# Another order of 1,135 steps in an attention, token-mix and MLP kernel

## The chip, the cores and the metric

One core of a Trainium2 chip runs the whole program as one launch. The metric is device time in microseconds (us) of one launch; before the change the median of three runs is 952.76 us (951.86 to 954.37). TensorE (PE) multiplies, VectorE (DVE), ScalarE (ACT) and GpSimd (POOL) do elementwise work, SyncE (SP) issues all DMAs. Each engine works off its own instruction stream strictly in order and waits on semaphores for the others.

## The reference

```python
scores = where(block_i >= block_j, q @ k.T / sqrt(64), -1e9)   # 4 batches, 8 heads, 576 x 64, blocks of 64
x  = softmax(scores) @ v                                       # -> 4 x 576 x 512
u  = x + (relu(x.T @ w_tok1) @ w_tok2).T                       # token mix, 576 -> 256 -> 576
u2 = u + relu(u @ w_ch1) @ w_ch2                               # MLP 1, 512 -> 1536 -> 512
out = u2 + relu(layernorm(u2) * g @ w_ch1') @ w_ch2'           # MLP 2, 512 -> 2048 -> 512
```

q, k, v are float32; the weights come as float64 and are taken apart into two planes on the chip.

## The kernel before

Every matmul operand is held as a high and a low plane, and each product is three passes (high x high, high x low, low x high). The 32 heads are worked in 16 pairs; two pairs make a quad (8 in all) of 256 columns, on which the token mix runs. `ORDER` is a string of words, each one step; `attention_and_token_mix` calls them one by one under a manual schedule, so the string alone sets the order of the instructions on every engine. A step's number is how often its word has come, or the number behind a colon. Later, `Mlps.run` has loops of its own for the rest of the two MLPs; they are not touched.

The words of one pair p: `lqk`, `lv` load q, k, v (SP). `rlk`, `rlq` copy k (ACT) and q (POOL) into the layout to transpose, `trk`, `trq`, `trr` transpose them on PE, `kh/qh/rmh` (ACT) and `kl/ql/rml` (DVE) write the two planes `kt`. `s3`, `s1`, `s02`, `s4` are the score matmuls by groups of row tiles, into PSUM tiles `ps` (two of them). `m*` is the row maximum (DVE), `n*` its negative (ACT), `e*` the exponential (ACT), `h*`, `l*` the two half-precision planes (POOL or DVE). `tA` and `tB` are DMA transposes of the planes of groups A (`s3`, `s1`) and B (`s02`, `s4`). `a3`, `a1` (from A), `a20`, `a4` (from B) multiply with v. `dn`, `ev`, `ev4` divide into `x`.

The words of one quad q: `xh` (ACT), `xl` (POOL) are the planes `xr` of x, `t1a`, `t1b` the first token matmul, `rh`, `rl` its planes, `t2a/b/c` the second, `ua/ub/uc` (DVE) add x, `us0`, `us1` store u to DRAM. `tl`, `td0` to `td3` load and split one of nine tiles of token weights (`td1` is four DVE operations). For the MLP: `bwl` loads a raw tile of weights, `bw0` takes its size (ACT), `bw1` rebases it (four DVE operations), `bc*` finds a scale, `bw2`, `bw3` write the planes. `bnl`, `ba`, `bk`, `bh`, `bo`, `bt` bring rows of u back and make their transposed planes; `b1` is one first-layer tile (PE), `br`, `bs` its planes.

PSUM tiles of `trk`, `trq`, `trr`, `cmm`, `a4`, `t1`, `t2` and most `b1` share three banks (`ps_mm`). SP, ACT, DVE and POOL never overtake within their stream: a step that waits holds up all behind it.

Of the kernel before, what the change touches and what calls it, by code (L numbers as in the profile page):

```python
# [43 lines left out]


ORDER = """
    lqk lv lt rlk rlq lv trk trq kh lqk abv kl qh cmm trr ql lv rmh rml cd1 s3 abv lt vh rlk rlq vl s1 m3 abv
    n3 cmm m1 trk e3 n1 cd1 trq lqk kh h3 trr e1 kl s4 l3 lv rmh h1 qh rml vh s02 m4 tl ql l1 vl tl rlk n4 rlq
    e4 tA s3 abv m02 td0 n02 td1 e02 lqk cmm trk m3 lv td0 h02 s1 kh n3 cd1 e3 h4 kl tl a3 l4 m1 td2 n1 vh td1
    s02 td3 e1 rlq l02 tl td2 abv td3 vl td0 h3 tB rlk td1 l3 trq td0 h1 trr lqk qh m02 s4 rmh td2 l1 n02 lv  # L50
    rml cmm e02 m4 a1 td3 ql a20 n4 cd1 tA e4 h02 td1 s3 vh h4 rlk l02 l4 td2 tl abv vl td3 s1 tl:6 m3 lv n3
    a4 m1 e3 n1 tl:5 dn ev e1 h3 s02 dn tB td0 l3 h1 td0:6 ev4 td1 abv td1:6 td2 l1 td0:5 a3 m02 td2:6 td3 tA
    s4 td3:6 n02 td1:5 e02 tl trk trq kh h02 m4 trr a1 qh tl a20 kl rmh n4 rlq td2:5 rml e4 a4 td3:5 ql lqk ev
    s3 h4 l02 bwl ev4 xh l4 s1 m3 a3 td0 xl tB trk n3 td0 m1 e3 trq n1 td1 trr a1 kh s02 rmh e1 rlq kl qh h3
    s4 td2 m02 rlk t1a td3 lqk n02 h1 e02 rml l1 bwl m4 t1b ql n4 l3 td1 e4 s3 dn td2 rh dn rlk rl s1 h02 tA
    m3 cmm a4 td3 h4 n3 t2a m1 e3 bwl l4 n1 cd1 l02 cmm a20 e1 h3 s02 ua vh tB l3 h1 ev cd1 a3 ev4 m02 vh t2b
    l1 n02 vl e02 t2c tA ub s4 uc vl trk h02 trq lv kh m4 trr a1 qh rlq a20 kl rmh n4 rml e4 a4 lqk ql ev h4
    s3 l02 l4 ev4 lv xh s1 m3 a3 abv xl us0 cmm n3 trk m1 e3 trq n1 cd1 a1 tB dn trr kh s02 rmh kl e1 rlq rml
    h3 qh t1a m02 abv l3 us1 vh n02 h1 s4 e02 ql t1b m4 l1 vl rlk h02 s3 tA rh rl n4 e4 a4 m3 lqk h4 t2a l4 n3
    l02 e3 s1 lv ua cmm a20 h3 m1 s02 n1 tB ev l3 e1 cd1 dn ev4 a3 h1 vh m02 t2b l1 rlk abv n02 vl s4 e02 tA  # L60
    ub t2c m4 trk uc trq n4 kh lv h02 trr a1 qh kl a20 rmh e4 rlq rml a4 ql h4 lqk ev s3 l4 l02 ev4 xh us0 s1
    m3 a3 xl abv tB cmm n3 trk m1 e3 trq n1 cd1 a1 dn trr kh s02 rmh kl e1 rlq us1 rml h3 qh t1a m02 vh l3 rlk
    n02 h1 lqk s4 e02 ql t1b m4 l1 vl h02 tA s3 rh rl n4 e4 rlq a4 m3 lv h4 t2a l4 n3 l02 e3 s1 ua cmm a20 h3
    m1 s02 tB n1 ev l3 e1 cd1 dn ev4 a3 h1 abv m02 t2b l1 vh n02 vl e02 t2c tA ub trk s4 uc kh h02 trq lv m4
    trr a1 qh kl n4 a20 rmh e4 rml a4 ql us0 rlk h4 ev s3 l4 l02 ev4 lqk xh s1 m3 a3 abv xl tB cmm n3 trk m1
    e3 trq n1 cd1 a1 dn trr kh s02 rmh kl e1 rlq us1 rml h3 qh t1a m02 vh l3 rlk n02 h1 lqk s4 e02 ql t1b m4
    l1 vl h02 s3 tA rh rl n4 rlq e4 a4 m3 h4 lv t2a l4 n3 l02 e3 s1 ua cmm a20 h3 m1 s02 tB n1 ev l3 e1 cd1 dn
    ev4 a3 h1 abv m02 t2b l1 vh n02 vl e02 t2c tA ub trk s4 uc kh h02 trq lv m4 trr a1 qh kl n4 a20 rmh e4 rml
    a4 ql us0 rlk h4 ev s1 l4 l02 ev4 s3 lqk xh m1 a3 n1 abv m3 xl tB cmm trk e1 trq n3 cd1 a1 kh dn trr s02
    e3 kl rlq us1 rmh h3 qh rml t1a m02 vh l3 rlk n02 h1 s4 lqk e02 ql t1b m4 l1 vl s3 h02 rh tA rl n4 rlq e4  # L70
    a4 m3 h4 lv t2a n3 l02 l4 e3 s1 ua cmm a20 h3 m1 s02 tB n1 ev l3 e1 cd1 dn ev4 a3 h1 abv m02 t2b l1 vh n02
    vl e02 t2c tA ub trk s4 uc kh h02 trq us0 m4 trr a1 qh kl n4 a20 rmh e4 rml a4 ql rlk h4 ev s3 lqk l4 l02
    ev4 xh s1 m3 us1 tB a3 xl cmm n3 trk m1 e3 trq n1 cd1 a1 dn trr kh s02 rmh kl e1 h3 rml qh t1a l3 h1 vh
    m02 rlk s4 n02 ql e02 l1 t1b m4 vl n4 tA rlq e4 s3 h02 rh dn h4 rl s1 m3 l4 t2a n3 m1 e3 cmm a4 ua n1 a20
    cd1 e1 h3 l02 s02 vh l3 h1 tB ev s4 m02 ev4 a3 l1 t2b n02 m4 e02 vl tA n4 t2c ub trk e4 uc trq kh trr us0
    dn h02 a1 rmh a20 kl qh h4 rml a4 ql l4 ev s3 l02 ev4 xh s1 m3 a3 us1 n3 a1 m1 tB bnl bnl bnl bnl bw0:0 e3
    n1 e1 xl s02 h3 s4 l3 h1 l1 tA t1a m02 n02 m4 bw1:0 e02 n4 t1b e4 h02 rh a4 h4 l02 l4 rl tB a20 ev4 ev dn
    t2a bw0:1 ba ba ba ba bw1:1 ua t2b ub t2c uc a3 a1 a20 a4 ev xh0 us0 us1 bk xl0 ev4 xh1 xl1 pc t1a bnl bnl
    bnl bnl bh bh bw0:2 bh bh bo bo bo bo bt bt bt bt bw1:2 t1b rh rl t2a bw0:3 bw1:3 bc1 ua t2b t2c bc2 ub uc
    us0 us1 op bnl bnl bnl bnl ba ba ba ba bk bc3 bw2 bw3 bw2 bw3 bw2 bw3 bw2 bw3 b1 br bh bh bo bo bt bt bs  # L80
    b1 br bh bh bo bo bt bt bs bw0:4 bw1:4 b1 br ba ba ba ba bs bk b1 br bh bh bo bo bt bt bs b1 br bh bh bo
    bo bt bt bs bw0:5 bw1:5 b1 br bs bw0:6 bw1:6 bnl bnl bnl bnl b1 br bs b1 br bs bw0:7 bw1:7 b1 br bc1 bs b1
    br bs bc2 b1 br bc3 bs bw2 bw3 bw2 bw3 ba ba ba ba b1 br bs bw2 bw3 bw2 bw3 bk
"""


class Net:
# [1043 lines left out]
```

## Time and profile before

| what | value |
|---|---|
| median of three runs | 952.76 us (951.86 to 954.37) |
| profiled execution | 954.12 us, span 952.3 us |
| mean granted TensorE clock | 0.966 of full |
| PE busy in the span | 881.7 us (93%) |
| DVE, ACT, POOL busy | 644.0, 352.4, 210.8 us |
| last exponentials of pair 15 | about 249 us |
| first `b1` matmul | 278.39 us |

Read it by stages. From about 330 us to the end PE works almost without a gap on the MLPs. Before, the span is the phase that `ORDER` sets. Times in the rows are microseconds from the start of the span; "<-" in a wait names what it waited for; a line number is that of the kernel before.

### The profile page before, as it was taken

The page shows a single profiled execution, that of the slowest core. Times are in us where ns is not written, and L with a number is a line of the kernel's source. Part 1 is how long each engine was busy: PE and PEld are TensorE (multiplying, and loading weights), DVE is VectorE, ACT ScalarE, POOL GpSimd, SP SyncE. Part 2 cuts the span into 40 slices and gives each one's busy share as a digit, 9 for nine tenths or more (in the row PEclk, how much of TensorE's full clock was granted, in tenths as well). Part 3 has the DMA queues.
Part 4 walks back from the last instruction along what each step waited for, and adds up shares of the span by engine and source line. Part 5 has one row for each costly group of instructions (what it writes and reads, how often), then busy time and mean ns, then how long its engine had stood idle before and what let it go on. Part 6 is the DMA issues. An engine that isn't in the chain of part 4 may idle for free.

```text
span 952.3 us, 15126 instructions
## 1 busy us (share of the span) xinstructions
PE 881.7 (93%) x5924; PEld 506.6 (53%) x5924; DVE 644.0 (68%) x1249; ACT 352.4 (37%) x847; POOL 210.8 (22%) x187
## 2 busy tenths in 40 slices
...
GB/s 201 183 202 178 208 201 207 163 215 156 202 207 220 81 167 86 76 58 89 67 44 51 83 89 67 111 45 45 45 44 45 23 1 1 1 1 10 58 56 77
DMA packets 193479, 96.66 MB, mean 102 GB/s; under 512 B 167744, under 2 KB 180800, under 8 KB 193408
## 3 DMA queue, kind: packets, MB, share of 16 engines
...
## 4 chain that ended last, share of the span: by engine, by line
PE 41%; issue 30%; POOL 2%; DVE 1%; ACT 0%; POOLq 0%
PE psy L984 21%; PE mm L947 20%; POOL pl L932 1%; POOL pl L931 1%; POOL vr L913 0%; POOL hlB L418 0%; DVE z L924 0%; ACT wide L398 0%; PE ps L333 0%; PE mm L812 0%; PE ps L363 0%; DVE diag L808 0%; DVE acc L988 0%; DVE mxf L801 0%; DVE mxf L802 0%
## 5 line engine op out<-in xcount | busy, mean ns | idle before, releaser
L947 PE MATMUL mm<-xt,w 128*128 128x512 f16 (+1 forms) x1680 | 335.5, 359 | 4.5 <-ACT w L848 2.6
L984 PE MATMUL psy<-w,hid 128*128 128x512 f16 x1512 | 335.5, 381 | 2.4 <-ACT w L848 2.0
L947 PEld LDWEIGHTS <-w 128*128 128x128 f16 x1680 | 164.6, 98 | 169.0 <-issue 4.4
L984 PEld LDWEIGHTS <-hid 128*128 128x128 f16 x1512 | 148.7, 98 | 180.5 <-issue 6.3
L958 ACT ACTIVATE hid<-mm 128x512 f16<-128x512 f32 (+1 forms) x140 | 77.3, 554 | 386.8 <-PE mm L947 386.7
L961 DVE SCALAR_TENSOR_TENSOR hid<-mm,hid 128x512 f16<-128x512 f32 (+1 forms) x140 | 87.9, 634 | 127.4 <-ACT hid L958 127.4
L988 DVE SCALAR_TENSOR_TENSOR acc<-psy,rg,acc 128x512 f32<-128x512 f32 x72 | 53.9, 750 | 87.5 <-PE psy L984 87.5
L333 PE MATMUL ps<-kt 64*128 64x512 f32 (+3 forms) x384 | 54.9, 402 | 17.8 <-ACT wide L398 16.0
L913 POOL TENSOR_TENSOR vr<-va,mhalf 128x4 f32<-128x4 f32 (+1 forms) x5 | 4.8, 961 | 298.9 <-DVE va L912 298.9
L398 ACT ACTIVATE wide<-ps,nm 128x512 f32<-128x512 f32 (+3 forms) x128 | 66.2, 527 | 3.2 <-issue 0.4
L772 ACT ACTIVATE w64a<-w 128x512 f32<-128x512 f32 x56 | 37.0, 668 | 69.2 <-DVE w L852 46.6
L988 DVE SCALAR_TENSOR_TENSOR acc<-psy,rs,acc 128x512 f32<-128x512 f32 x54 | 40.0, 748 | 22.1 <-PE psy L984 20.8
L422 POOL TENSOR_TENSOR hlA<-wide,hlA 128x1024 f16<-128x1024 f32 (+1 forms) x32 | 53.0, 1662 | 7.1 <-DVE hlA L418 5.8
L375 DVE TENSOR_REDUCE mx<-ps 128x2 f32<-128x768 f32 (+2 forms) x64 | 49.9, 813 | 3.0 <-PE ps L338 3.0
L546 PE MATMUL mm<-xr,wt 128*128 128x256 f32 (+1 forms) x240 | 45.7, 350 | 5.3 <-DVE kt L304 3.0
L333 PEld LDWEIGHTS ps<-kt 64*128 64x128 f32 x384 | 38.0, 227 | 23.1 <-ACT wide L398 17.8
L546 PEld LDWEIGHTS mm<-xr,wt 128*128 128x128 f32 (+1 forms) x240 | 40.3, 246 | 9.7 <-DVE kt L304 3.8
L789 DVE SCALAR_TENSOR_TENSOR w64a<-w,w64a 128x512 int32<-128x512 int32 x56 | 41.1, 735 | 1.9
L787 DVE SCALAR_TENSOR_TENSOR w64a<-w,w64a 128x512 int32<-128x512 int32 x56 | 39.4, 703 | 1.9
L782 DVE TENSOR_SCALAR_CACHE_REDUCE w64a<-w64a 128x512 f32<-128x512 f32 x56 | 37.8, 675 | 0.2
L304 DVE TENSOR_TENSOR kt<-ptr,kt 128x512 fp32r<-128x512 f32 (+1 forms) x48 | 26.4, 572 | 16.5 <-ACT kt L306 16.2
L569 PE MATMUL mm<-h,wt 128*128 128x256 f32 (+1 forms) x240 | 33.3, 289 | 2.3 <-DVE h L558 1.6
(128 smaller groups left out, 941.3 us busy)
## 6 DMA issues: line engine op xcount, KB each, us to landing
...
```

What stands on the lines that cost most here:

```text
L333: nc.tensor.matmul(views[hh], kt[r, a, KQ + t * P : KQ + (t + 1) * P], kt[r, c, KK : KK + n], start=i == 0, stop=False)
L375: nc.vector.tensor_reduce(s["mx"][:, c : c + 2], ps, axis=AX.X, op=ALU.max)
L398: nc.scalar.activation(d[:, g, sl], s["ps", key][:, g, sl], AF.Exp, scale=SCALE, bias=s["nm"][:, c + g : c + g + 1], accum_out=s["rs"][:, ...
L422: (nc.vector if last else on("l" + key)).tensor_tensor(lo_, src, hi, ALU.subtract)
L546: nc.tensor.matmul(s["ps1"][:, m], w1[:r, t, a, m * P : (m + 1) * P], s["xr"][:r, c, t], start=i == 0, stop=i == 3 * NT - 1)
L787: nc.vector.scalar_tensor_tensor(ai, raw[:, :, 1], -0x40000000, ai, ALU.bitwise_and, ALU.bitwise_or)
L789: nc.vector.scalar_tensor_tensor(ai, raw[:, :, 0], 29, ai, ALU.logical_shift_right, ALU.bitwise_or)
L947: self.nc.tensor.matmul(self.ps[h].rearrange("p (t n) -> p t n", n=P), W[:, a, h * P : (h + 1) * P], self.xt[b][:, :, 4 * c + k], start=i ...
L958: self.nc.scalar.activation(hid[:, 0, :w], ps, AF.Relu)
L961: self.nc.vector.scalar_tensor_tensor(hid[:, 1, :w], ps, 0.0, hid[:, 0, :w], ALU.max, ALU.subtract)
L984: self.nc.tensor.matmul(y, self.hid[v, h][:, a, k * P : (k + 1) * P], W[:, c], start=i == 0, stop=i == 11)
L988: self.nc.vector.scalar_tensor_tensor(self.acc[j], y, self.ps["r", v][k], self.acc[j], ALU.mult, ALU.add)
```

## The change

The 1,128 words of `ORDER` become 1,135 and stand in another order, many with explicit numbers. All steps that were there stay. The seven new words are `bwl:3` to `bwl:9`: before, `bw1:i` loaded tile i+2 behind its own DVE work. Some lines change so that steps of a kind may come in any order. Two lines of the string, and the rest of the diff:

```diff
-    dn h02 a1 rmh a20 kl qh h4 rml a4 ql l4 ev s3 l02 ev4 xh s1 m3 a3 us1 n3 a1 m1 tB bnl bnl bnl bnl bw0:0 e3
+    kl us1 n02 qh m4 bnl rml ql dn e02 n4 a4 e4 l3 s1 uc ev4 m1 a20 s3 n1 ev tA e1 s4 us1 xh m3 h4 a1 dn
...
@@ def tr / def pl
-            if "kt" not in s:
-                s["kt"] = p2.tile([P, 2, 1216], F32R, name="kt", bufs=BUFS["kt"])
...
+            if "kt" not in s:
+                s["kt"] = p2.tile([P, 2, 1216], F32R, name="kt", bufs=BUFS["kt"])
...
-            "bw1": lambda i: (first.rebase(i), i and first.load(i + 2)),
+            "bw1": first.rebase,
...
-        if k == 0:
+        if s not in self.mx:
             self.mx[s] = self.small([P, 4], "mx4", 3)
...
-        if k == 0:
-            self.nrm[b] = self.small([P, 4], "nrm", 3)
+        if b not in self.nrm:
+            self.nrm[b] = self.small([P, 4], "nrm", 4)
...
-        self.ps[h] = ps[:, : n * P]
+        ps = self.ps[v, h] = ps[:, : n * P]
...
-        ps = self.ps[h]
+        ps = self.ps[v, h]
```

The line numbers of the kernel after are higher by 5 behind the string (by 3 in `tr`).

SP, the first loads of the program. Before:

```order
L210 DMA rawq_119<-in_q_dram 128x2x256
L210 DMA rawq_119<-in_k_dram 128x2x256
L221 DMA rawv_120<-in_v_dram 128x4x64 x2
L223 DMA rawv_120<-in_v_dram 64x2x64
L230 DMA ktail<-in_k_dram 64x8x64
L233 DMA qtail<-in_q_dram 64x4x64 x2
L221 DMA rawv_121<-in_v_dram 128x4x64 x2
L223 DMA rawv_121<-in_v_dram 64x2x64
```

And now:

```order
L113 DMA w_138<-in_moe_w_tok_dram 128x512
L215 DMA rawq_119<-in_q_dram 128x2x256
L215 DMA rawq_119<-in_k_dram 128x2x256
L235 DMA ktail<-in_k_dram 64x8x64
L238 DMA qtail<-in_q_dram 64x4x64 x2
L226 DMA rawv_121<-in_v_dram 128x4x64 x2
L228 DMA rawv_121<-in_v_dram 64x2x64
L226 DMA rawv_122<-in_v_dram 128x4x64 x2
```

The first tile of token weights (`tl`) stands ahead of q and k, and the tails of q and k (`lt`, for `trr`) ahead of v; v of pair 1 comes before v of pair 0.

ACT, from the last softmax work ahead of quad 2's `xh` (the two rows of `xr`; `L495`, now `L500`, is `ev4`, `L306`/`L311` copies into `kt`, `wide` the exponentials). Before:

```order
L383 ACTIVATE nm<-mx,lnp 128x1
L306 ACTIVATE kt<-ptr 128x512 x2
L306 ACTIVATE kt<-ptr 128x192
L389 ACTIVATE p_0_130,rs<-ps,nm 128x576
L495 ACTIVATE x<-x_1862,den 64x64 x2
L526 ACTIVATE xr<-x 128x1024
L526 ACTIVATE xr<-x 64x256
```

And now:

```order
L394 ACTIVATE p_0_130,rs<-ps,nm 128x576
L500 ACTIVATE x<-x_1845,den 64x64 x2
L311 ACTIVATE kt<-ptr 128x512
L388 ACTIVATE nm<-mx,lnp 128x2
L403 ACTIVATE wide,rs<-ps,nm 128x512 x2
L531 ACTIVATE xr<-x 128x1024
L531 ACTIVATE xr<-x 64x256
```

Between `ev4` and `xh` stand now a plane of q (`qh:8`), `n3:7` and the two exponentials of `e3:7`.

DVE, the last pair and quads 6 and 7 (`mx` are maxima, `w64a` the rebases `bw1`, `h_...` is `rl:6`, `x<-xps` is `ev`). Before:

```order
L375 TENSOR_REDUCE mx<-ps 128x2 x2
L373 TENSOR_REDUCE mx<-ps 128x1
L782 TENSOR_SCALAR w64a,mx_4104<-w64a 128x512
L785 TENSOR_SCALAR w64a<-w64a 128x512
L787 SCALAR_TENSOR_TENSOR w64a<-w_858,w64a 128x512
L789 SCALAR_TENSOR_TENSOR w64a<-w_858,w64a 128x512
L422 TENSOR_TENSOR hlB<-wide,hlB 128x1024
L422 TENSOR_TENSOR hlB<-p_1_131,hlB 128x640
L558 SCALAR_TENSOR_TENSOR h_4133<-mm,h_4133 128x512
L487 TENSOR_TENSOR x<-xps,den 128x4x128
```

And now:

```order
L787 TENSOR_SCALAR w64a,mx_4053<-w64a 128x512
L790 TENSOR_SCALAR w64a<-w64a 128x512
L792 SCALAR_TENSOR_TENSOR w64a<-w_903,w64a 128x512
L794 SCALAR_TENSOR_TENSOR w64a<-w_903,w64a 128x512
L378 TENSOR_REDUCE mx<-ps 128x1
L380 TENSOR_REDUCE mx<-ps 128x2 x2
L563 SCALAR_TENSOR_TENSOR h_4107<-mm,h_4107 128x512
L787 TENSOR_SCALAR w64a,mx_4053<-w64a 128x512
L790 TENSOR_SCALAR w64a<-w64a 128x512
L792 SCALAR_TENSOR_TENSOR w64a<-w_1273,w64a 128x512
L794 SCALAR_TENSOR_TENSOR w64a<-w_1273,w64a 128x512
L492 TENSOR_TENSOR x<-xps,den 128x4x128
```

One rebase stands now ahead of the maxima of `s4:15` and `s02:15`, a second between `rl:6` and `ev:14`, and `l02:15` (`hlB`) behind them. In all, four rebases (`bw1:0` to `bw1:3`) stand ahead of `ev:15` on DVE, where two did.

Where PE multiplies with v: between the later of `s3`, `s1` of a pair and the first of its `a3`, `a1`, the string has 25.7 other PE steps on the mean over pairs 5 to 14, and had 16.3. Between `s3` and the score step that takes its PSUM tile it has 7.0, and had 6.1. Between `t2b` and the third step behind it that takes one of the three shared banks it has 7, 6, 4, 4, 4, 3, 5, 3 in quads 0 to 7, and had 3, 3, 3, 3, 3, 2, 5, 2. Between the last `a` step of a quad and its `t1a` the two steps `a3` and `a1` of the next pair stood in quads 0 to 6; now they stand there in none (in quad 6 `a1:14` alone).

## Rows read from the trace of the kernel before

**Rows 1.** The page, busy time of TensorE (share of the span, instructions).
```profile
PE 881.7 (93%) x5924; PEld 506.6 (53%) x5924; DVE 644.0 (68%) x1249; ACT 352.4 (37%) x847; POOL 210.8 (22%) x187
```

**Rows 2.** Busy us of each engine in five stretches, clock, DMA share.
```profile
core 0: us, PE busy (x) PEld busy (x) DVE busy (x) ACT busy (x) POOL busy (x), PEclk, DMA share, GB/s
0.00:20.00 20.00, 12.12 (x60) 9.05 (x60) 9.52 (x27) 12.35 (x29) 8.56 (x18) 1.00 0.93 196
20.00:100.00 80.00, 56.97 (x679) 48.86 (x679) 76.79 (x120) 54.86 (x166) 52.71 (x45) 0.83 0.86 190
100.00:236.00 136.00, 118.51 (x1629) 103.74 (x1631) 115.12 (x186) 103.48 (x316) 101.08 (x78) 0.95 0.92 190
236.00:278.40 42.40, 31.93 (x341) 28.02 (x341) 33.55 (x71) 23.26 (x60) 9.05 (x8) 0.84 0.89 217
278.40:330.00 51.60, 46.74 (x205) 20.32 (x206) 39.49 (x86) 28.39 (x55) 0.00 (x0) 0.97 0.60 154
```

**Rows 3.** Waits of TensorE, 100 to 236 us: total, times, longest.
```profile
PE ps L333 <- ACT wide L398: 6.7, 4, 2.0
PE ptr L103 <- DVE u L579: 5.6, 6, 2.1
PE xps L449 <- DMA ptA<-hlA: 3.9, 3, 1.6
```

**Rows 4.** Timeline of the start: start, duration, instruction, idle time before it.
```profile
4.21 0.62 POOL L272 TENSOR_SCALAR sc<-rawq 128x512 f32<-128x512 f32 x1
4.56 0.63 ACT L270 ACTIVATE sc<-rawq 128x512 f32<-128x512 f32 x1 [2.35 <-DMA rawq<-in_k_dram]
5.33 1.94 PE L103 MATMUL ptr<-ident,sc 128*128 128x128 f32 x8 [5.33 <-ACT sc L270]
8.62 1.65 PE L333 MATMUL ps<-kt 64*128 64x512 f32 x6
```

**Rows 5.** Timeline, the first VectorE work of pair 0.
```profile
7.09 0.69 DVE L304 TENSOR_TENSOR kt<-ptr,kt 128x512 fp32r<-128x512 f32 x1 [5.35 <-ACT kt L306]
```

**Rows 6.** Timeline of TensorE around quad 2's first token-mix matmul.
```profile
126.09 0.87 PE L449 MATMUL xps<-vt,ptA 128*128 128x64 f16 x24 [1.50 <-DMA ptA<-hlA]
127.74 0.51 PE L449 MATMUL xps<-vt,ptA 128*128 128x64 f16 x12
129.84 0.80 PE L333 MATMUL ps<-kt 64*128 64x384 f32 x6 [1.12 <-ACT wide L398]
131.24 0.50 PE L546 MATMUL mm<-xr,wt 128*128 128x256 f32 x2
```

**Rows 7.** Timeline of VectorE, ScalarE, GpSimd: what feeds that matmul.
```profile
123.18 0.68 DVE L487 TENSOR_TENSOR x<-xps,den 128x512 f32<-128x512 f32 x1
123.89 1.37 ACT L526 ACTIVATE xr<-x 128x1024 fp32r<-128x1024 f32 x2
126.21 3.03 POOL L534 TENSOR_TENSOR xr<-x,xr 128x1024 fp32r<-128x1024 f32 x2
```

**Rows 8.** Waits of VectorE, 236 to 279 us, and two timeline rows.
```profile
DVE mx L375 <- PE ps L338: 2.6, 1, 2.6
DVE x L487 <- PE xps L449: 1.6, 1, 1.6
...
254.10 0.63 DVE L782 TENSOR_SCALAR_CACHE_REDUCE w64a<-w64a 128x512 f32<-128x512 f32 x1
...
278.39 0.61 PE L947 MATMUL mm<-xt,w 128*128 128x512 f16 x2 [2.57 <-ACT w L848]
```

**Rows 9.** VectorE rows with GpSimd beside; line 418 (min/median/max ns, first and last).
```profile
22.73 0.28 DVE L126 TENSOR_SCALAR w64a<-w64a 128x256 f32<-128x256 f32 x1
27.16 1.40 DVE L126 TENSOR_SCALAR w64a<-w64a 128x256 f32<-128x256 f32 x1
27.01 1.40 POOL L422 TENSOR_TENSOR hlB<-p,hlB 128x640 f16<-128x640 f32 x1
...
L418 DVE TENSOR_SCALAR hlA<-wide x15: 380/864/2306, 17.1 to 227.9; 128x512 f16<-128x512 f32 x15
```

More of the change, by code (lines that the diff above doesn't have):

```diff
@@ L46 @@
 ORDER = """
[L47 to L75, printed above, removed]
-    dn h02 a1 rmh a20 kl qh h4 rml a4 ql l4 ev s3 l02 ev4 xh s1 m3 a3 us1 n3 a1 m1 tB bnl bnl bnl bnl bw0:0 e3
@@ L77 @@
[L77 to L81, printed above, removed]
@@ L82 @@
-    bo bt bt bs bw0:5 bw1:5 b1 br bs bw0:6 bw1:6 bnl bnl bnl bnl b1 br bs b1 br bs bw0:7 bw1:7 b1 br bc1 bs b1
-    br bs bc2 b1 br bc3 bs bw2 bw3 bw2 bw3 ba ba ba ba b1 br bs bw2 bw3 bw2 bw3 bk
+    tl lqk td0 lt rlq trq qh lv:1 trr rlk ql lv:2 lqk rmh rml lv:0 trk kh kl rlq abv:1 rlk s3 s1 td1 tl:3
+    lqk m3 n3 e3 trr m1 trk rmh trq s4 s02 m4 n1 kh abv:2 e1 abv:0 cmm:1 rlk qh cmm:0 trk tl:1 kl rml m02
+    n4 td0 h3 td0:3 ql rlq e4 cd1 n02 h1 s1 td1:3 s3 tl:2 vh trq l1 e02 lqk cd1 l3 m1 vl kh s02 h4 m3 n1
@@ new lines @@
+    trr rlq kl td2:3 td2:0 lt n3 tl e1 tl:8 vh rlk h02 trk e3 td1:1 m02 qh s4 l02 l4 h1 ql s1 td3:3 h3 n02
+    td0:4 td0:2 e02 tA lqk lv trq m4 l1 n4 td1:2 l3 e4 td3:0 td2:1 h02 td1 qh tB s3 rlq m1 kh kl m3 rmh
+    dn:1 n1 e1 td2:2 s02 rml a1 tl cmm ql abv s4 n3 cd1 trr a20 td2 e3 a3 rlk vl td0:6 h1 h4 m02 cmm td1:6
+    tl:5 m4 l02 rmh l4 h3 a4 td0:8 tA s3 tB n02 dn:0 td1:8 e02 n4 tl:7 td3:1 a3 ev4 td2:8 vh a20 l3 m3 s1
+    rml a1 e4 cd1 vl a4 l1 h4 ev l4 trq lv vh n3 s4 td0:5 dn td1:5 e3 ev ev4 m1 xh vl lqk h02 trk td3:8 n1
@@ new lines @@
+    l02 td0:7 trr e1 kh td1:7 h1 rlq qh m4 bwl ql lv td3:2 td2 td2 abv n4 rmh cmm td3:4 tB h3 xl cd1 td2:5
+    rml abv kl s02 l1 t1a e4 td3 s3 rlk t1b m02 s1 vh n02 a4 e02 m3 l3 dn rh tA h4 a1 a20 h02 n3 cmm ev4
+    rl td3:5 trq m1 cd1 e3 lqk rlq s4 qh trk n1 e1 l4 lv l02 vl td3:7 a3 m4 h3 kh tA h1 s02 n4 e4 t2a kl
+    ql t2b s3 m02 ev rlk abv a1 n02 ub e02 l1 tB bwl:2 a4 vh m3 a20 s02 l3 trq n3 h4 ua l4 m02 lqk a3 ev
+    cmm ev4 h02 e3 qh s1 trr rmh xh ql vl n02 l02 bw0:2 e02 m1 rml t2c trk cd1 rlq lv xl s4 trq m4 t1a t1b
@@ new lines @@
+    abv rlk h3 vh uc vl cmm kh n1 bw0:0 lv kl trk tB dn us1 tA n4 s1 qh e1 abv ql rh a20 a4 h1 trr cd1 lqk
+    l1 e4 rl kh bwl:1 s3 h02 m1 t2b a1 l3 n1 trr kl m3 rmh h4 tA e1 h1 trr n3 ub ev4 rml rmh l02 l4 rml
+    s02 s4 m02 rlq a3 t2a e3 tB h3 rlk a1 n02 l1 l3 lqk rmh m4 trk vh trq a3 rml e02 s3 ev ua a4 n4 a20 vl
+    lv:10 dn s1 kh kl m3 ev e4 ev4 qh h4 n3 lv:9 h02 e3 t2c s4 xh m1 l4 cmm rlq n1 s02 l02 m4 tA ql rlk s1
+    cd1 xl e1 n4 h1 e4 abv t1a vh m02 t1b vl cmm abv tB n02 uc e02 m1 l1 dn lqk us0 rh s3 rl lv m3 h4 a20
@@ new lines @@
+    t2a s02 n1 h02 a4 e1 h3 l02 dn cd1 trq n3 ua m02 trk ev4 l3 l4 e3 kh t2c tA a1 kl n02 h3 qh a3 ql rlk
+    e02 l3 cmm cd1 uc s4 t2b abv vh s3 m4 rlq trr:10 ev trr:9 a3 tB n4 us1 h1 ub e4 h4 rmh:10 m3 cmm n3 a1
+    vl h02 s1 us0 a4 cd1 a20 s02 rml:10 lv trq m1 rmh:9 e3 n1 ev vh:11 ev4 trk l1 xh rml:9 lqk l02 kh s4
+    l4 xl m02 qh h3 ql tA rlq us1 e1 m4 l3 kl rlk trk h1 t1a abv n02 s3 e02 t1b n4 vh:10 s1 trq dn vl:11
+    m3 tB e4 h02 kh a20 h4 rh l4 a1 kl a4 qh a3 rl n3 l1 m1 cmm s02 t2b lqk s4 t2a n1 l02 vl:10 e3 trr ql
```

20 lines of the change are left out of this document (19 added, 1 removed).

## The prediction

> **What bounds the kernel now.** I read the busy times first: PE is busy for 881.7 us of the span [rows 1], which says only that the long MLP stretch is full. The table by stretches says more [rows 2]. From 0 to 330 us PE does 266.3 us of work, so it stands still for 63.7 us: 7.9 in the first 20 us, 23.0 from 20 to 100, 17.5 from 100 to 236, 10.5 from there to the first `b1`, 4.9 behind it. Nothing else can be won, since behind 330 us the program is the same and PE is full. In the stretches where PE waits, another engine is nearer to full: from 20 to 100 us DVE is busy for 76.79 of 80 us, from 100 to 236 for 115.12 of 136, and the DMA engines for 0.92 of the time. Then I read what PE waits for in the middle [rows 3]: a score PSUM tile that the exponentials have not yet read (6.7 us), a shared bank that `u` has not yet been read from (5.6), the DMA transpose of group A (3.9). Last I read DVE's waits in the tail, and the timeline of the start [rows 4, 5, 8].
>
> Every engine does the same work in both kernels; the new string adds no wait of its own. So the sum is one of stalls, stretch by stretch, against the profiled execution (954.1 us); the median of the three runs is 1.4 us below it.
>
> **The change, part by part.**
>
> *The start.* Before, the two relays run side by side, k's on ACT from 4.56 us, and `s3:0` starts at 8.62 [rows 4]. Now ACT has `qh:0` ahead of k's relay. q's relay ends at about 4.21 + 0.5 (the issue of the token weights put ahead) + 0.62 = 5.3; four of the eight transposes (1.94 us for eight) take 1.0; `qh`, of the size of a relay, 0.63; so k's relay starts at 6.9, 2.4 us later than 4.56. Behind it only four transposes are left, not eight, so 1.0 comes back. The first scores come 1.4 us later. Bounds: 0 (VectorE finds other work meanwhile) and 3 us (the tails of q and k, needed by `trr` ahead of `trk`, land late). I take +1.5.
>
> *DVE's first 20 us and the stretch it bounds.* DVE is busy for 9.52 of the first 20 us; its first real work starts at 7.09 [rows 2, 5]. So 3.4 us are idle that filling could use. The new string puts `td1:0`, four DVE operations on token weights, ahead of the first maximum, and `td1:3` shortly behind it. The stretch behind is bound by DVE (96% busy), so what is done earlier shortens it. Bounds: -3.4 and 0. I take -3.0.
>
> The Trainium skill, Perfetto Trace Analysis, section Identifying the Most-Contended Engine, says that the engine with the highest occupancy should be made cheaper first. By it an order alone, which takes no work from DVE, wins nothing from 20 to 100 us; the sum below would be 3.0 higher. The 96% agree with the rule inside that stretch; the work I count as won comes from ahead of it.
>
> *The middle, 100 to 236 us.* The score tiles: between `s3` and the taker of its tile stand 7.0 PE steps instead of 6.1, but three of ten pairs still have five or fewer; before, five of ten had exactly five. So three fifths of 6.7 us stay: -2.7. The shared bank: four of the five quads here have more steps than before between `t2b` and the third taker, one has three as before: four fifths of 5.6, -4.5. The transposes: 25.7 PE steps between scores and their `a` steps instead of 16.3; all of 3.9 goes. Together -11.1.
>
> What is late next is `t1a`. In quad 2 it starts at 131.24 [rows 6], while `xr` is complete at 126.21 + 3.03 = 129.24 [rows 7], 2.0 us to spare. Two waits ahead of it, 1.50 and 1.12 us, go by the count above, and the two steps `a3` and `a1`, 0.87 and 0.51, no longer stand there: PE comes 4.0 us earlier, and waits 2.0 of them. The chain to `xr` can shorten by about 1 us: from `ev` at 123.18, 0.7 to `xh`, then 1.37 and 3.03 without the gap in which POOL worked on `hlB`, makes 5.1 where 6.1 passed. So a new wait of 1.0 to 2.0 us for each quad; it can also be nothing where PE comes late anyway. I take 1.0, as the ACT steps now ahead of `xh` do not need `ev` and can run while it is awaited. Five quads lie here: +5.0. The middle gives -6.1. Bounds: 136 us x 0.08 = 10.9 is all that the DMA engines leave at their present packets, so -10.9; above, the wait of 2.0 in each quad and half of the gains, -5.5 + 10 = +4.5.
>
> *The tail, 236 us to the first `b1`.* `b1` waits at 278.39 for the weights' planes [rows 8], so for DVE, which does 33.55 us of work in 42.4 [rows 2]. Of its 8.9 us of idle time, 2.6 are one wait for the last scores and 1.6 one for the last product with v [rows 8]. A rebase takes four operations of about 0.63 us, 2.5 in all, and two more of them now stand ahead of `ev:15`; each covers one of these waits: -4.2. DVE's work up to the first `b1` is the same set of steps but for one rebase more (`bw1:4` instead of none), which the rest of its idle time takes. Bounds: -8.9 (no idle left) and +2.5 (the extra rebase is paid in full). I take -4.2.
>
> *The first `b1` to 330 us.* PE idles for 4.9 us there for weight scales and planes. The last rebases are mixed with `bo` and `bs` as before. Bounds -3 and +3; I take 0. The separate `bwl` steps move raw loads within SP's queue: a load there is issued when its buffer is free, and now it no longer waits behind DVE's rebase in the string alone. They cost SP the same issue; 0, covered as DMA is busy for 0.60 there. The changed tile and dictionary lines add no instruction.
>
> Sum: 954.1 + 1.5 - 3.0 - 6.1 - 4.2 = 942.3; 1.4 less is 940.9 us.
>
> **The rivals.**
>
> *The DMA engines set the pace of the middle.* For it: 0.92 busy over 136 us [rows 2]. Against: packets of a busy engine stretch, and PE's waits on DMA are only 3.9 of 17.5 us. Then neither the middle nor the stretch ahead of it shrinks: 954.1 + 1.5 - 4.2 - 1.4 = 950.0, no change.
>
> *`t1a` waits longer (slower).* Place: ACT's queue between `ev4` and `xh`, where quad 2 now has a plane of q and two exponentials (the order of ACT above). Should they not be done when `ev` comes, they cost some 3 x 0.63 = 1.9 us at the price of a copy [rows 4] on top of the 2.0 above. Then each of seven quads loses 3.9 instead of 1.0: +20, 961. It decides from 1.7 us more per quad, (952.8 - 940.9) / 7. For it: PE has no step with v left there. Against: exponentials of that pair are due before, and a wait there lets the other engines get ahead.
>
> *DVE loses less to GpSimd.* The same `td1` operation took 0.28 us at 22.73 and 1.40 at 27.16, where a POOL operation ran from 27.01 to 28.41 [rows 9]; line 418 on DVE (`h1`) has a median of 0.864 and a minimum of 0.380. If the new order put its 15 instructions where POOL idles, 15 x 0.484 = 7.3 us more go: 933.6. It can as well go the other way by as much, 948.2.
>
> The Trainium skill, SBUF — State Buffer, section Who interferes with whom, says that VectorE in its two-port modes and GpSimd take one shared port pair for a whole instruction, and whichever comes second is blocked. The pair of rows agrees (the blocked operation ends at 28.56, 0.15 us behind POOL's). By it these 7.3 us depend on neighbours in time that no string fixes, so I give either sign a part in the range, not in the sum.
>
> **How the numbers follow.** The forecast has 0.56, the DMA rival 0.13, `t1a` 0.13, the port rival 0.14, and 0.04 is left for a tail that is longer. A run of this kernel can tell a change from none at about 0.3%, 2.9 us. Faster: 0.56 + 0.14 = 0.70; same 0.13; slower 0.13 + 0.04 = 0.17. The likeliest case alone reaches from 932 to 949. The range goes from 922 (the port rival and a middle at its DMA bound: 940.9 - 7.3 - 4.8 - 4.7 of the tail is 924) to 959, just short of the slower rival; about 0.07 lies below and 0.12 above.
>
> **What would show it.** Right: `s3:0` at about 10 us; DVE busier in the first 20 us; in the middle no waits of PE on `u` and on the transposes, less on the exponentials, and a new one of `t1a` on `xr` of about 1 us in each quad; first `b1` at some 266 us; PE full from there but for some 5 us. Wrong: a first `b1` at 275 us or later; waits of `t1a` beyond 2.7 us; a DMA share that rises to 1.0 over the middle without a shorter middle; or the tail's gain given back between `b1` and 330 us.

## The result and the profile after

The new order is slower: 961.21 us median of five runs against 952.76, ratio 1.0089 (95% interval 1.0064 to 1.0113). The forecast, 940.9 us and faster, was wrong in sign, and the time lies above its range.

The profiled execution took 958.68 us with a span of 956.9. First the page's busy times, to be laid beside [rows 1]: the work is the same, PE's sum is 1.6 us longer and VectorE's 5.7 us shorter.

```profile
PE 883.3 (92%) x5924; PEld 508.7 (53%) x5924; DVE 638.3 (67%) x1249; ACT 348.8 (36%) x847; POOL 209.3 (22%) x187
```

Then the table by stretches, the last two cut at the new first `b1`, 291.5 us, in place of 278.4 [rows 2].

```profile
0.00:20.00 20.00, 11.09 (x60) 7.99 (x60) 8.56 (x24) 11.92 (x31) 6.44 (x17) 1.00 0.79 202
20.00:100.00 80.00, 51.81 (x618) 43.34 (x619) 69.34 (x113) 52.14 (x159) 52.48 (x45) 0.70 0.79 170
100.00:236.00 136.00, 118.44 (x1551) 101.81 (x1548) 107.92 (x177) 101.07 (x305) 94.97 (x74) 0.91 0.96 190
236.00:291.50 55.50, 45.18 (x490) 39.52 (x486) 47.34 (x93) 32.51 (x84) 16.02 (x12) 0.75 0.89 192
291.50:330.00 38.50, 38.50 (x182) 17.70 (x181) 29.20 (x68) 18.93 (x40) 0.00 (x0) 1.00 0.66 168
```

VectorE, to be filled in the first 20 us, is busy for 8.56 us of them where it was for 9.52, and from 20 to 100 us for 69.34 where it was for 76.79: the engine that bound this stretch now waits in it. From 100 to 236 us PE idles for 17.6 us, as before (17.5). Behind the first `b1` PE is full, where it had idled for 4.9 us.

PE's waits from 100 to 236 us (total, times, longest), against [rows 3]:

```profile
PE ps L368 <- ACT wide L403: 3.8, 4, 2.3
PE xps L454 <- DMA ptA<-hlA: 3.2, 2, 2.2
PE ps L338 <- ACT wide L403: 2.2, 3, 1.8
PE ptr L108 <- DVE kt L309: 2.1, 2, 1.8
PE mm L574 <- DVE h L563: 1.7, 1, 1.7
PE ptr L108 <- DVE eb L259: 1.6, 2, 1.4
PE mm L574 <- DVE kt L309: 1.4, 2, 0.9
PE mm L551 <- DVE u L584: 0.4, 1, 0.4
PE ptr L108 <- DVE u L584: 0.3, 1, 0.3
```

The wait on `u`, 5.6 us, fell to 0.7 as forecast. The waits on the exponentials only went from 6.7 to 6.0 us, those on the transposes from 3.9 to 3.2. The waits on `kt`, `eb` and `h` take 6.8 us now, and PE's idle time is the same.

How late the program is, read from the timelines (start in us; `b1:11` is the twelfth `b1` to run; the rows e1 to e4 are spliced orders, below):

| kernel | `t1a` quad 0 | quad 1 | quad 5 | `tB:15` | first `b1` | `b1:11` | end |
|---|---|---|---|---|---|---|---|
| before | 74.0 | 102.2 | 216.6 | 253.0 | 278.4 | 312.0 | 952.3 |
| after | 79.9 | 108.9 | 222.6 | 265.9 | 291.5 | 320.2 | 956.9 |
| e1: new to step 907, then old | 81.2 | 110.5 | 226.7 | 267.2 | 293.9 | 326.1 | 964.1 |
| e2: old to step 907, then new | 73.8 | 101.8 | 215.6 | 254.6 | 278.2 | 306.9 | 945.7 |
| e3: new to step 301, then old | 81.1 | 109.2 | 223.0 | 259.5 | 284.9 | 318.6 | 956.6 |
| e4: old to step 331, then new | 74.0 | 106.6 | 220.6 | 265.8 | 291.8 | 320.5 | 957.2 |

Three things stand in it. The new start costs 6 to 7 us by `t1a` of quad 0 and keeps them. Quad 1 to quad 5 takes 113.7 to 114.4 us in five of the six, whatever the order. From `t1a` of quad 5 to `tB:15` it is 36.4 us before and 43.3 after, but from the first `b1` to `b1:11` 33.6 before and 28.7 with the new tail. Behind it stands a gap of PE: from the first `b1` to 330 us it idles for 4.8 to 5.1 us in the profiles of all runs with the old tail (2.6 in e1) and not at all in the twelve with the new one. These are single profiles: e1 and the new kernel have the same order up to step 907 and yet differ by 6 us at `s3:15` (250.9 and 244.9), so differences under some 4 us are not read from the table; the medians below decide.

### The profile page after: what moved, and what is told of

The parts are those of the page before. It is cut to its first block, busy times and chain, and to the rows that moved or that the text cites. A ratio compares the mean times of both kernels' runs of the same rounds, so it can differ in the third digit from the quotient of the medians.

```text
span 956.9 us, 15108 instructions
## 1 busy us (share of the span) xinstructions
PE 883.3 (92%) x5924; PEld 508.7 (53%) x5924; DVE 638.3 (67%) x1249; ACT 348.8 (36%) x847; POOL 209.3 (22%) x187
## 4 chain that ended last, share of the span: by engine, by line
PE 41%; issue 32%; DVE 5%; POOL 4%; DMA 2%; ACT 2%; POOLq 0%; SPq 0%; ACTq 0%
PE psy L989 18%; PE mm L952 17%; PE mm L551 2%; POOL pl L937 2%; PE ps L338 1%; POOL pl L936 1%; ACT wide L403 1%; DVE mx L380 1%; DMA ptA<-hlA 1%; PE mm L574 1%; PE xps L454 1%; DMA ptB<-hlB 1%; PE ptr L108 1%; POOL vr L918 1%; DVE xr L539 0%
## 5 line engine op out<-in xcount | busy, mean ns | idle before, releaser
L427 POOL TENSOR_TENSOR hlA<-wide,hlA 128x512 f16<-128x512 f32 (+1 forms) x32 | 55.6, 1745 | 16.9 <-DVE hlA L423 16.4
L380 DVE TENSOR_REDUCE mx<-ps 128x2 f32<-128x768 f32 (+3 forms) x64 | 50.8, 815 | 11.8 <-PE ps L343 11.7
L574 PE MATMUL mm<-h,wt 128*128 128x256 f32 (+1 forms) x240 | 36.3, 304 | 4.5 <-DVE h L563 2.0
L454 PE MATMUL xps<-vt,ptA 128*128 128x64 f16 x576 | 23.4, 200 | 13.9 <-DMA ptA<-hlA 8.5
```

The lines of the kernel that those rows point to most:

```text
L380: nc.vector.tensor_reduce(s["mx"][:, c : c + 2], ps, axis=AX.X, op=ALU.max)
L427: (nc.vector if last else on("l" + key)).tensor_tensor(lo_, src, hi, ALU.subtract)
L574: nc.tensor.matmul(ps[:r, k], w2[:, m, a, t * P : t * P + r], s["h1"][:, c, m], start=i == 0, stop=i == 5)
```

## Experiments

Ratios are to the kernel before, run on the same chip (952.85 to 953.9 us there).

**Where: orders spliced at two cuts.** The first n steps of one order, then the steps left, as the other order has them.

```diff
-ORDER = new
+ORDER = new[:907] + [w for w in old if w not in new[:907]]   # e1
+ORDER = old[:907] + [w for w in new if w not in old[:907]]   # e2
+ORDER = new[:301] + [w for w in old if w not in new[:301]]   # e3
+ORDER = old[:331] + [w for w in new if w not in old[:331]]   # e4
```

e1. 

> The first 907 steps in the new order (up to the scores of pair 15, near 240 us), the other 228 in the order they had before. Theory T (the tail: the loss of some 7 us between 236 us and the first b1 comes from the new order of the last pair and of the rebases): 961.2 - 7 = 954, first b1 some 7 us earlier than 291.5. Theory E (the start: the loss is made before the first t1a, which is 5.9 us later, and the tail only hands it on): the loss up to there stays and the tail gives nothing, 960 to 961.

965.72 us, 1.0146 (1.0114 to 1.0177): slower than the whole change.

e2. 

> The first 907 steps in the old order, the rest in the new one. Theory T: 952.8 + 7 = 960, first b1 near 285. Theory E: the tail is as good as the old one, 952 to 954, first b1 near 278.

949.66 us, 0.9970 (0.9937 to 1.0004). Theory T falls in both: with the new tail the kernel is 4.5 us faster (new start and middle) and 3.5 us faster (old ones). The second difference alone is not clear of noise, since its interval reaches 1; the first just is, as the intervals of e1 and of the whole change do not overlap.

e3. 

> The first 301 steps in the new order (up to the scores of pair 5, near 95 us), the rest in the old one. Theory E: quad 0's t1a at about 80 us and the delay of 5.9 us stays to the end, 958 to 959. Theory T: the middle takes most of the delay back, since its waits absorb it, 953 to 955.

959.55 us, 1.0070 (1.0033 to 1.0108): the start alone costs 6.4 us.

e4. 

> The first 331 steps in the old order, the rest in the new one. Theory E: 961.2 - 5.9 = 955, with the t1a of quad 0 at 74 us. Theory T: as slow as the whole change, 959 to 961. If the new order's middle is really 6 us shorter, as was forecast, t1a of quad 5 comes at about 210 us instead of 216.6.

961.88 us, 1.0111 (1.0075 to 1.0148): as slow as theory T had it, though its tail is the one that gains. `t1a` of quad 5 comes at 220.6, not at 210, so the new middle is not shorter. With the tail's -3.5 the new middle costs 12.2 us behind the old start. e1 and e3 give 6.2 for it, and the whole change (961.21 against the 953.14 of these runs) 8.1 - 6.4 + 3.5 = 5.2. A splice has a seam of its own (quad 0 to quad 1 takes 32.6 us in e4, 28.2 before), so the middle's price is 5 to 12 us, not a sharper number.

**The start.** VectorE's and GpSimd's rows of the new kernel between 21 and 29 us, one timeline each:

```profile
21.57 0.29 DVE L131 TENSOR_SCALAR w64a<-w64a 128x256 f32<-128x256 f32 x1
21.89 1.22 DVE L133 TENSOR_SCALAR w64a<-w64a 128x256 int32<-128x256 int32 x1
23.14 2.23 DVE L135 SCALAR_TENSOR_TENSOR w64a<-w,w64a 128x256 int32<-128x256 int32 x1
25.41 0.82 DVE L137 SCALAR_TENSOR_TENSOR w64a<-w,w64a 128x256 int32<-128x256 int32 x1
...
26.60 0.68 DVE L380 TENSOR_REDUCE mx<-ps 128x2 f32<-128x512 f32 x1
```

```profile
21.80 3.29 POOL L427 TENSOR_TENSOR hlA<-wide,hlA 128x512 f16<-128x512 f32 x2 [4.97 <-DVE hlA L423]
```

```profile
27.31 0.30 ACT L388 ACTIVATE nm<-mx,lnp 128x2 f32<-128x2 f32 x1 [2.82 <-DVE mx L380]
```

```profile
30.81 0.69 PE L338 MATMUL ps<-kt 64*128 64x384 f32 x2 [3.99 <-DVE w64a L133]
```

The scores of `s1:1` are complete at 23.1 us. VectorE is busy with `td1:3`, token weights that `t1a` is the first to need, at 79.9 us, and three of its four operations, beside GpSimd, take 1.22, 2.23 and 0.82 us where the next such step, from 30.05 us, takes 0.29, 0.42 and 0.42. The maximum `m1:1` starts at 26.60, ACT waits 2.82 us for it, and PE 3.99 us for a free score tile. (The row names `w64a`; the later release is `e1:1` on ACT, done at 30.8.)

The longest wait of the start comes later, for a plane that stands on VectorE behind another such split, `td1:7`:

```profile
77.73 0.16 PE L254 MATMUL pt<-ab,ones 128*128 128x1 bf16 x1 [9.34 <-DVE kt L309]
```

e9 moves this split.

```diff
-... td1:7 h1:3 rlq:5 qh:4 m4:3 ... kl:4 ...
+... h1:3 rlq:5 qh:4 m4:3 ... kl:4 td1:7 ...
```

> The new order with one word moved: the VectorE split td1:7 (token weights that only t2 of quad 0 needs) stands behind kl:4 instead of ahead of it. In the new kernel TensorE stood still for 9.34 us ahead of cmm:4 because kl:4 was queued on VectorE behind td1:7, one operation of which took 4.41 us beside GpSimd's work. Theory K (that queue is a part of the start's loss): the wait falls to 3 to 5 us, t1a of quad 0 comes at 75 to 77 us instead of 79.9, and the total is 957 to 958. Rival: xr is complete only at about 75.5 us and the loss comes back as other waits behind it: t1a at 78 to 80, 960 to 962.

962.05 us, 1.0089 (1.0063 to 1.0114). The wait fell from 9.34 to 6.57 us, `t1a` came at 79.4, and nothing was gained: the rival's outcome.

e5 takes up SyncE's queue.

```diff
-... tl:4 e1:1 tl:8 ... e02:1 tA:0 ...          +... tA:0 tl:4 e1:1 tl:8 ...
-... a1:0 tl:6 ... tl:5 m4:2 l02:1 ... tA:1    +... a1:0 tA:1 tl:6 ... l02:1 cd1:2 ...
-... l1:2 ... tB:2 ... tA:2                    +... l1:2 tA:2 ...
```

> The new order with five words moved, all in its first 200: the transposes tA:0, tA:1 and tA:2 stand ahead of raw loads or transposes that wait (tA:0 started at 32.2 us though its planes were complete at 25.1; tA:2 at 73.2, complete at 54.6), and l02:1 ahead of cd1:2, so that tB:1 need not wait till 57. Theory Q (SyncE's queue: the start lost its 6 us because transposes stood behind waiting loads and the DMA engines had holes): most of the 6 us comes back, 955 to 957, t1a of quad 0 at 74 to 76 us, DMA share from 20 to 60 us up from 0.68. Theory V (VectorE: its waits for late scores made the loss, the transposes had slack): 960 to 962, t1a at 79 to 81.

959.00 us, 1.0058 (1.0034 to 1.0081). The DMA share from 20 to 60 us rose from 0.68 to 0.81, `t1a` came at 78.6. That is some 2 of the 6 us and between the two theories; the intervals of this run and of the whole change overlap, so theory Q is not shown.

e12 and e13 move the 45 steps `tl`, `td0` to `td3` alone.

```diff
+e12: new order; each tl/td step stands behind as many other steps as in the old order
+e13: old order; each tl/td step stands behind as many other steps as in the new order (td3:7 alone 15 fewer)
```

> The new order, with the 45 token-weight steps (tl, td0 to td3) where the old order had them: each stands behind as many other steps as there. Theory P (priority: the start loses because VectorE, which is never idle there, splits token weights early and so takes the maxima late; TensorE's work is 5.9 us late by 40 us while VectorE's sum of work is on time): the lag at 60 to 100 us goes, t1a of quad 0 at 74 to 76 us, 954 to 957 in all. Rival (the relays, tails and loads at the very start, or the places of kl, rml and l02, make the loss): t1a at 79 to 82, 959 to 962.

965.65 us, 1.0121 (1.0094 to 1.0147), `t1a` at 85.1: worse still. The early splits are not the whole of the loss.

> The reverse: the old order, with the 45 token-weight steps where the new order has them. Theory P: TensorE 5 to 6 us late by 60 us, t1a of quad 0 at 79 to 80, 958 to 960 in all. Rival: t1a at 74 to 76, 952 to 955.

959.18 us, 1.0056 (1.0035 to 1.0076), `t1a` at 81.7: by themselves they cost the old order 5.6 us, nearly what the whole new start costs it (6.4). Theory P holds for e13 and fails in e12: either the start's other moves lose as well, or they do not go with the splits in their old places; these two runs do not say which. e16 and e17 cut the start in two.

```diff
+ORDER = new[:52] + [w for w in old if w not in new[:52]]     # e16
+ORDER = new[:110] + [w for w in old if w not in new[:110]]   # e17
```

> The first 52 steps in the new order (up to m02:0, near 20 us), the rest in the old one. Forecast's terms for this piece: +1.5 (k's relay behind qh) - 3.0 (VectorE filled) = 951 to 952. Theory F (the first 20 us already make the loss: v of pair 0 comes behind v of pairs 1 and 2, and POOL and the transposes are late from there): 957 to 959, t1a of quad 0 near 79. Theory G (it is made between 20 and 60 us by the token-weight splits): 952 to 955.

956.39 us, 1.0029 (1.0005 to 1.0052), between the two theories. Where the forecast's terms for this piece make 1.5 us less, it takes 2.5 us more.

> The first 110 steps in the new order (up to e02:1, near 35 us), the rest in the old one. Theory G: 957 to 959, and more than the run with 52 by 4 us or more. Theory F: no more than 2 us above the run with 52 steps.

960.17 us, 1.0064 (1.0040 to 1.0089). The first 20 us cost some 2.5 us, the 15 behind them 3.8 more, just under theory G's 4, and then the start's loss is complete. The rows from 21 to 31 us lie in that piece; that `td1:3` alone makes it was not tried.

The clock is a rival here. Before, it is granted at full (2.4 GHz) for nearly all of the time from 20 to 40 us; in the new kernel it falls to half (1.2 GHz) at 20.1 us, after PE was busy for 3.13 of 5 us (for 3.92 in the kernel before, where it stays at full), and remains there to 40 us. The rows are those of before, of the new kernel and of e17:

```profile
20.00:40.00 20.00, 12.81 (x110) 10.12 (x110) 19.51 (x31) 13.83 (x43) 12.19 (x12) 0.94 0.89 208
```

```profile
20.00:40.00 20.00, 12.72 (x68) 9.76 (x70) 18.28 (x30) 14.26 (x46) 13.61 (x11) 0.50 0.70 138
```

```profile
20.00:40.00 20.00, 10.60 (x67) 8.09 (x63) 17.62 (x31) 13.49 (x44) 11.22 (x9) 0.99 0.64 117
```

e17 has the new order there, ran at 0.99 and got no further, 67 matmuls against 68. So up to 40 us the low clock is not what costs; from there on the profiles do not settle it.

**The middle.** e6 (new order) and e7 (old) leave out the low planes' transposes.

```diff
-                out=pt.rearrange("p a b t -> p (a b) t"),
-                in_=s["hl"][g].rearrange("p a w -> p (a w)"))
+                out=pt[:, 0], in_=s["hl"][g][:, 0])
...
-                                s["xps"][:, t, hh, :], pt[:, a, hh * per + off + j, :],
+                                s["xps"][:, t, hh, :], pt[:, 0, hh * per + off + j, :],
```

> The new order; the DMA transposes move the high planes alone and the products with v read these in place of the low planes, so the output differs by the low planes' part. No step is moved. Theory D (the DMA engines pace the middle, 0.96 busy): the stretch from t1a of quad 1 to t1a of quad 5, 113.7 us, shrinks to the next bound, 100 to 106 us, and the start loses less; 940 to 950 in all. Theory V (VectorE paces): 112 to 114 us as before, 958 to 961.

> The same with the old order: high planes alone are transposed and read twice. Theory D: t1a of quad 1 to t1a of quad 5 from 114.4 to 100 to 106 us, 938 to 946 in all, and the difference between the orders at the start, 6 us, gets smaller. Theory V: 112 to 114 us, 950 to 953.

e6: 960.89 us, 1.0098 (1.0062 to 1.0133); e7: 944.12, 0.9909 (0.9881 to 0.9937). The stretch 100 to 236 us, of e6 and then of e7:

```profile
100.00:236.00 136.00, 120.45 (x1581) 104.65 (x1578) 108.79 (x184) 101.98 (x307) 97.39 (x75) 0.92 0.64 136
```

```profile
100.00:236.00 136.00, 123.55 (x1679) 108.18 (x1677) 117.86 (x191) 105.80 (x319) 103.24 (x79) 0.92 0.64 135
```

The DMA share falls to 0.64, and quad 1 to quad 5 from 113.7 to 108.4 us (new) and from 114.4 to 109.5 (old): 5 us in either order, though not the 8 to 14 of theory D. In all profiles with whole transposes this stretch takes 111.8 to 117.0 us. In the old order the median follows; in the new one it does not.

The edit frees more than the DMA engines. The transposes issued in the 136 us (20, in e6 21) keep SyncE busy for 84.7 us in both orders and for 38.7 in e6. And a transpose that reads the high planes alone no longer has to wait for the steps `l*`: SyncE's waits for them in this stretch fall from 33.9 us in the new kernel to 2.8 in e6. Which of the three gives the 5 us was not tried.

e8 relieves VectorE.

```diff
-                ps = s["ps", key][:, :, sl]
+                w = (sl.stop - sl.start) // 2
+                ps = s["ps", key][:, :, sl.start : sl.start + w]
```

> The new order; each row maximum is taken over the first half of its columns alone, which takes about 1.6 us of VectorE's work off each pair (half of 1.2, 0.68, 1.36 and 0.75 less the fixed part), 3.3 off each quad, and changes what the exponentials hold. Theory V: t1a of quad 1 to t1a of quad 5 from 113.7 down by up to 13, to 101 to 106, and in all 945 to 950. Theory D: 112 to 114 us there; only the stretches outside the DMA engines' pace gain, 957 to 961.

961.22 us, 1.0080 (1.0053 to 1.0108); VectorE is busy for 96.49 of the 136 us instead of 107.92, and quad 1 to quad 5 takes 113.2. Theory V falls: VectorE's sum of work does not set the middle's pace.

> The new order, with both reliefs at once: only the high planes are transposed (and read in place of the low ones), and each maximum is taken over half of its columns; the output differs by these parts. Half the transposes alone took t1a of quad 1 to t1a of quad 5 from 113.7 to 108.4 us, half the maxima alone left it at 113.2. Theory M2 (two bounds side by side, the DMA engines first and VectorE right behind): 100 to 104 us. Rival (the chain of steps from engine to engine is what remains): 106 to 109 us. In all 953 to 958 by either, as the start and the tail keep their losses.

950.51 us, 0.9960 (0.9936 to 0.9985). Quad 1 to quad 5 takes 107.6 us, as with the transposes alone (the rival). But in all it is 10.7 us below the new kernel, more than either theory had: each relief alone gave nothing in the median, both together do. `t1a` of quad 0 comes at 74.6, so part of it is the start. Why the two add up to more than their sum was not found.

e10 and e11 hold the clock up: some TensorE steps repeat their own matmuls where PE would idle.

```diff
+FILL = {'t2c:0': 2, 't2c:1': 1, 'cmm:8': 8, 'trk:10': 3, 'a20:9': 2, ...}
...
                 ALL[k](i)
+                for f, a, w in log * FILL.get(f"{k}:{i}", 0):
+                    f(*a, **w)
```

> The new order; nine TensorE steps that stand ahead of a long idle time in its trace (t2c:0, t2c:1, cmm:8, trk:10, a20:9, trq:14, s4:15, a4:14, t2a:6) repeat their own matmuls once to eight times, with the same values into the same PSUM tile: some 12 us of added TensorE work for some 18 us of idle time between 100 and 277 us. Theory C (the clock: the same 2,706 matmuls ahead of the first b1 take 226.7 us of TensorE here and 219.5 before, because the clock falls to half behind these holes, ahead of t1a): the clock stays at 1.00 in more of the stretch, the matmuls that are not repeats take 219 to 222 us, total 954 to 958. Rival (the low clock only fills time that is idle anyway): the added work costs what it takes beyond the holes, 961 to 968.

964.03 us, 1.0115 (1.0092 to 1.0138). From 100 to 236 us the clock rose from 0.91 to 0.99 and quad 1 to quad 5 took 115.8 us:

```profile
100.00:236.00 136.00, 115.20 (x1628) 99.19 (x1624) 108.06 (x174) 100.03 (x302) 94.03 (x74) 0.99 0.95 186
```

Theory C falls for the new order: the higher clock did not pay for the repeats. So its slower matmuls (226.7 us for those ahead of the first `b1`, 219.5 before) lay, as far as this net result shows, in time that PE would have waited through. The repeats begin behind 100 us; the start was not tried.

> The old order up to step 907 and the new tail (949.7 us), with the same kind of repeats in nine steps ahead of its own long idle times (trr:6, s1:7, s4:8, trr:10, trr:12, s1:13, a1:14, a4:14, t2a:6; some 12 us of work for 19 us of idle time). Theory C: the low-clock stretches at 100, 125, 150, 160, 185 and 255 to 275 us shorten, 944 to 948, faster than both kernels. Rival: 950 to 956.

945.91 us, 0.9920 (0.9898 to 0.9942), as theory C had it for this order; faster than both kernels, by 7.9 us than the one before. From 100 to 236 us the clock is 0.99, where it is 0.94 in e2. Against e2 it is 3.7 us, and their intervals just overlap.

**The tail.** e14 is e2 with two early rebases (`bw1:0`, `bw1:2`) moved back; e18 is the old order with its first two (`bw1:0`, `bw1:1`) moved ahead.

```diff
-... s02:15 bw1:0 ... m4:15 m02:15 ... rl:6 bw1:2 ... l02:15 ...
+... s02:15 ... m4:15 m02:15 bw1:0 ... rl:6 ... l02:15 bw1:2 ...      # e14
-... m02:15 n02:15 m4:15 bw1:0 ... rh:6 a4:14 h4:15 l02:15 ... bw0:1 ... bw1:1 bwl:3
+... bw1:0 m02:15 n02:15 m4:15 ... rh:6 bw0:1 bw1:1 bwl:3 a4:14 h4:15 l02:15 ...   # e18
```

> The old order up to step 907 and the new tail, as in the run of 949.7 us, with two rebases moved back on VectorE: bw1:0 from ahead of m4:15 to behind m02:15, bw1:2 from ahead of l02:15 to behind it. Theory R (the forecast's: early rebases fill VectorE's waits, and this is the tail's gain): a part of the 3.5 us is lost, 951 to 953. Theory T2 (they hold up the last pair, and the gain comes from the order behind it, where planes and rows no longer keep b1 waiting): tB:15 comes 2 to 4 us earlier than at 254.6, total 946 to 949.

953.27 us, 1.0001 (0.9975 to 1.0027): 3.6 us lost, as theory R had it (the interval overlaps that of e2), and `tB:15` came at 260.8, not earlier. Half of that lateness stands there ahead of the first moved step (`t1a` of quad 5 at 218.9, in e2 at 215.6), so the medians decide. PE has no gap behind the first `b1` here either; what e14 loses, it loses ahead of it.

> The old order with only the first two rebases moved on VectorE: bw1:0 from behind m4:15 to ahead of m02:15, bw1:1 (with bw0:1 and bwl:3) from behind dn:15 to ahead of l02:15. If rebases ahead of the last pair's work are what the new tail gains by (forecast: -4.2): 949 to 951, first b1 at 274 to 276 us. Rival (they only gain together with the later steps in their new order, or hold up pair 15): 953 to 956, tB:15 later than 253.0.

959.69 us, 1.0061 (1.0036 to 1.0087): two moves of the same kind in the old tail lose 5.8 us. PE's longest wait from 236 to 330 us there (total, times, longest), and the start of the second rebase:

```profile
PE mm L592 <- DVE h L581: 5.3, 1, 5.3
```

```profile
251.11 0.69 DVE L805 TENSOR_SCALAR_CACHE_REDUCE w64a<-w64a 128x512 f32<-128x512 f32 x1 [3.79 <-ACT w64a L795]
```

`t2` of quad 6 waits for `rl:6`, which VectorE does late: ahead of it in the queue stand `bw1:1` and two steps `l*` of pair 15, and `bw1:1` itself waits 3.79 us for `bw0:1`, which stands on ACT behind pair 15's exponentials. So an early rebase loses where its own input comes late; e18 does not show what it gains where the input is there. What the new tail gains shows in PE's waits behind the first `b1`. In e3, which has the old tail, 278 to 330 us:

```profile
PE mm L970 <- ACT w L871: 2.6, 1, 2.6
PE psy L1007 <- ACT w L871: 2.0, 1, 2.0
PE mm L970 <- DVE a4s L845: 1.6, 1, 1.6
PE mm L835 <- DVE diag L831: 0.7, 1, 0.7
```

From its first `b1` to 330 us, the new kernel (as e2) has none to show. Its first `b1` follows `t2` without a pause, where it had waited 2.57 us for the planes [rows 8]:

```profile
288.79 2.88 PE L574 MATMUL mm<-h,wt 128*128 128x256 f32 x19
291.51 2.76 PE L952 MATMUL mm<-xt,w 128*128 128x512 f16 x12
```

## Why the prediction was wrong

*The start (+1.5) and VectorE's first 20 us (-3.0): the step that failed first.* The relay's part was right: `s3:0` starts at 9.77 us where it was 8.62 [rows 4], forecast some 10.

```profile
9.77 1.95 PE L338 MATMUL ps<-kt 64*128 64x512 f32 x6 [0.69 <-ACT kt L311]
```

The rest was not. The forecast took VectorE's work as a sum that may be done in any order: what fits into early idle time shortens the bound stretch. But VectorE's first 20 us held 0.96 us less work, not 3 more. `td1:0` did run in them, from 10.36 us, but v of pair 0, of which VectorE wrote a plane there before (0.88 us), now comes later, and VectorE waits for scores:

```profile
16.97 0.76 DVE L378 TENSOR_REDUCE mx<-ps 128x1 f32<-128x576 f32 x1 [3.06 <-PE ps L368]
```

And where the splits do run early they stand ahead of maxima on whose result ACT, PE and the transposes wait. The stretch was bound by VectorE and by the chain through it. Together -1.5 was forecast and +6.4 measured (e3), of which 2.5 fall in the first 20 us (e16). That the early splits suffice for such a loss is shown by e13; that they make all of it in the new order is not, since e12, without them, is slower still. The idle time was misread too, but that weighs little: behind 7.09 us VectorE idles for 4.2 us of the first 20, not 3.4, as the 9.52 us hold 0.8 from ahead of it.

*The middle (-6.1): the term with the wrong model.* It added up PE's waits and took each as time won. The waits on `u` went (-4.9, forecast -4.5); those on the exponentials and the transposes fell by 0.7 us each, where -2.7 and -3.9 were forecast; others took their place, and PE's idle time stayed, 17.5 and 17.6 us. Two counts behind the terms are off by one as well: four of the ten pairs, not three, have five or fewer steps, and quad 5 rose from two steps to three. Quad 1 to quad 5 takes 114 us in both, and 5 less where half of the transposes' work is gone (e6, e7). That is in part what the first rival, to which the forecast gave 0.13, would make of the middle; whether the DMA engines set the pace, or SyncE, which each transpose holds for 3.5 to 6.5 us, or the low planes that it waits for, these runs do not tell apart. The forecast's own new wait did not come either: `t1a` of quad 2 starts without one (and of the eight only quad 1's has a wait, 0.4 us for `u`), though `xr` is complete only at 134.29 + 3.22 = 137.51 us [rows 6, 7].

```profile
134.29 3.22 POOL L539 TENSOR_TENSOR xr<-x,xr 128x1024 fp32r<-128x1024 f32 x2 [1.57 <-ACT xr L531]
```

```profile
139.17 6.04 PE L551 MATMUL mm<-xr,wt 128*128 128x256 f32 x30
```

So the second rival, 961 us, met the time and not the cause. Though quad 1 to quad 5 takes no longer, the new middle costs 5 to 12 us by the splices. In the table it shows at its ends: `t1a` of quad 5 to `tB:15` takes 4.1 us longer in e1, which has the old tail, than before. Why was not tried.

*The tail (-4.2).* The size was right, -3.5 and -4.5 by e2 and e1; the place was not. VectorE's idle time was filled about as forecast: in e2 it is busy for 37.58 of the 42.4 us to 278.4, and was for 33.55 [rows 2].

```profile
236.00:278.40 42.40, 30.00 (x331) 26.32 (x328) 37.58 (x74) 25.92 (x64) 9.51 (x7) 0.84 0.88 210
```

But the forecast moved the first `b1` up. It is at the same time in e2 as before, 278.2, and the gain comes behind it, in the 4.9 us that it had counted as 0 ("The first `b1` to 330 us"). That the number agrees is luck to that extent.

*GpSimd beside VectorE.* Summed over VectorE's instructions ahead of the first `b1` (389 and 394), the time above the shortest of each operation and shape fell from 54.7 to 49.3 us, the third rival's direction and most of its size [rows 9]. It bought nothing: by the tables of stretches VectorE's idle time ahead of the first `b1` rose from 43.4 to 58.3 us.

In sum: start +6.4, tail -3.5, and the whole +8.1 leave +5.2 for the middle, where -1.5, -4.2 and -6.1 were forecast. So the loss lies in the start and the middle; what costs in the middle stays open.
